# A feed-forward block on one core: x loaded plainly in 32-partition strips and transposed by VectorE in 32x32 blocks

## The chip, the core and the metric

The kernel runs on one NeuronCore of a Trainium2 chip. The metric is the device time of one execution, in microseconds (us). A profiled execution leaves a trace of every instruction; its "span" runs from the first to the last instruction. Engines are TensorE (PE: matmuls, with its weight loads shown apart as PEld), VectorE (DVE), ScalarE (ACT), GpSimd (POOL) and SyncE (SP, which here only issues DMAs and waits). Each engine works through its own instructions in order and waits for others by semaphores.

## The reference

```
x: 1 x 2048 x 512, w_gate and w_up: 512 x 1376, w_down: 1376 x 512, all bf16
g = silu(x @ w_gate)
u = x @ w_up
return (g * u) @ w_down
```

S = 2048 tokens, D = 512, F = 1376. A matmul on TensorE contracts over partitions, so for the first two products x has to stand in SBUF with D on the partitions, that is, transposed; D is cut into four slices of 128, numbered dk.

## The kernel before, in words

**Tiles.** The tokens are worked on in four chunks c of 512 (SC). F is cut into ten full tiles of 128 (ft = 0 to 9) and a rest of 96. For each chunk and each full tile there is a pair of groups: G (gate) and U (up), each of four 128x512 matmuls (dk = 0 to 3) that accumulate in one of eight PSUM banks. ScalarE turns a finished G bank into silu in SBUF; VectorE multiplies that by the finished U bank and writes the product to hT_sb. After the ten pairs of a chunk comes one group X of four matmuls (gate rest and a part of the up rest, L325), with two silus and one product. After all chunks, two groups Y do what is left of the up rest, and then 16 groups O multiply hT_sb by w_down (L353), one per 128 tokens; VectorE copies each O bank out and SyncE stores it.

**Order.** The order is written out by hand. Planning functions (plan_pair, plan_x, plan_y) append groups to one list, which TensorE works through, and append operations to act_ops and dve_ops, which ScalarE and VectorE work through strictly in that order. Every VectorE operation raises the semaphore s_D by one, so a wait for "operation n of VectorE" is a wait for all operations before it too. Before a group may write its bank, the readers of the group eight places earlier must be done (free). A weight slab or a piece of x is waited for by its own DMA semaphore (need).

**Loads.** SyncE issues, in this order: the first 256 tokens of x as two plain loads into xn_sb (tokens on partitions); tokens 256 to 511 ("x0b") as a DMA transpose straight into xT_sb (load_x, L79); the weight slabs from tile 1 on, each as a gate part and an up part (load_w, L84), of 1, 2, 3 and 4 tiles; the rest of w_up; chunks 1 to 3 of x, one DMA transpose each; w_down in two loads. ScalarE issues slab 0 (wg0 and wu0) before its table load. Row d of a weight goes to partition d % 128, slice d // 128 ("(k p) f").

**The head.** TensorE starts with four dummy matmuls of 512 columns on constants (warm, L296). GpSimd builds an identity. As the two plain pieces of x arrive, TensorE transposes them with the identity (L304, two 128x128 blocks to a bank), and VectorE (slices 0 and 1) and ScalarE (slices 2 and 3) copy the banks into xT_sb. Three dummies of 128 columns follow, and then the first pair is worked in pieces of tokens as they are there: 128, 128, then 256.

Of the kernel before, what the change touches and what calls it, by code (L numbers as in the profile page):

```python
# [5 lines left out]
ALU = mybir.AluOpType  # L6
BF16 = mybir.dt.bfloat16
FP32 = mybir.dt.float32

N_WARM = 4  # L10
N_FILL = 3


def bass_standalone__swiglu_ffn__prompt_kernel(nc, x, w_gate, w_up, w_down, out):
    _, S, D = x.shape
    F = w_gate.shape[1]
    P = 128
    KD = D // P
    NFF = F // P
    NFT = NFF + 1  # L20
    F_LAST = F - NFF * P
    SC = 512
    NSC = S // SC
    TPC = SC // P
    NST = S // P
    LASTA = 384
    HT = SC // 2
    NXN = HT // P
    NB = 8
    NSG = 4  # L30
    NOS = 3
# [2 lines left out]
    xf = x[0]  # L34
# [3 lines left out]
    UPH = F + 32  # L38
# [4 lines left out]
    with ExitStack() as es:  # L43
        sb = lambda name, shape, dt: es.enter_context(nc.sbuf_tensor(name, shape, dt))
        ps = lambda name, shape, dt: es.enter_context(nc.psum_tensor(name, shape, dt))
        sem = lambda name: es.enter_context(nc.semaphore(name))
# [9 lines left out]
        o_sb = [sb(f"o_sb{i}", [P, D], BF16) for i in range(NOS)]  # L56
        banks = [ps(f"bank{i}", [P, 512], FP32) for i in range(NB)]

        xn_sb = sb("xn_sb", [P, NXN, D], BF16)
        ident = sb("ident", [P, P], BF16)  # L60

        s_I = sem("s_I")
        s_P = sem("s_P")
        s_A = sem("s_A")
        s_D = sem("s_D")
# [3 lines left out]
        def load_sem(name):  # L69
            loads[name] = sem(f"s_{name}")  # L70
            return loads[name]
# [3 lines left out]
        zero_c = nc.const_aps.tensor(0.0, [P, 4], FP32)  # L75


        def load_x(eng, name, t0, t1):
            eng.dma_start_transpose(  # L79
                xT_sb[:, :, t0:t1], xf[t0:t1, :]  # L80
            ).then_inc(load_sem(name), 16)

        def load_w(eng, name, src, base, f0, f1):
            eng.dma_start(  # L84
                w_sb[:, :, base + f0:base + f1],
                src[:, f0:f1].rearrange("(k p) f -> p k f", p=P),
            ).then_inc(load_sem(name), 16)

        slabs = [(0, 1), (1, 2), (2, 4), (4, 7), (7, NFT)]
# [2 lines left out]
        def load_slab(eng, a, b):  # L92
            load_w(eng, f"wg{a}", w_gate, 0, a * P, min(b * P, F))
            load_w(eng, f"wu{a}", w_up, UPH, a * P, min(b * P, F - 32))

        def loads_on_scalar(act):
            load_slab(act, *slabs[0])

        def loads_on_sync(sp):
            for i in range(NXN):  # L100
                sp.dma_start(xn_sb[:, i, :], xf[i * P:(i + 1) * P, :]).then_inc(load_sem(f"xn{i}"), 16)
            load_x(sp, "x0b", HT, SC)
            for a, b in slabs[1:]:
                load_slab(sp, a, b)
            load_w(sp, "wut", w_up, F - (F - 32), F - 32, F)
            for c in range(1, NSC):
                load_x(sp, f"x{c}", c * SC, (c + 1) * SC)
            sp.dma_start(
                wd_sb[:, 0:NFF, :], w_down[0:NFF * P, :].rearrange("(k p) d -> p k d", p=P)
            ).then_inc(load_sem("wd"), 16)  # L110
            sp.dma_start(wd_sb[0:F_LAST, NFF, :], w_down[NFF * P:F, :]).then_inc(load_sem("wdt"), 16)
# [7 lines left out]
        def add_group(kind, **what):  # L119
            g = dict(kind=kind, at=len(groups), bank=banks[len(groups) % NB], readers=[], **what)  # L120
            groups.append(g)
            return g

        def add_op(eng, g, **what):
            n_read[eng] += 1
            op = dict(g=g, at=n_read[eng], **what)
            (act_ops if eng == "A" else dve_ops).append(op)
            g["readers"].append((eng, op["at"]))
            return op

        def tview(bank):
            return bank[:, 0:P].bitcast(BF16).rearrange("p (k t) -> p k t", k=2)

        sg_reader = []
        n_sg = 0
        h_ready = {}
# [1 line left out]
        def plan_pair(c, ft):  # L138
            nonlocal n_sg
            gg = add_group("G", c=c, ft=ft)  # L140
            gu = add_group("U", c=c, ft=ft)
            b = n_sg % NSG
            free = sg_reader[n_sg - NSG] if n_sg >= NSG else 0
            a = add_op("A", gg, kind="silu", out=sg_sb[b][:, :], src=gg["bank"][:, :], free=free)
            d = add_op(
                "D", gu, kind="mul", out=hT_sb[:, ft, c * SC:(c + 1) * SC], a=sg_sb[b][:, :],
                b=gu["bank"][:, :], after=a["at"],
            )
            sg_reader.append(d["at"])
            h_ready[c] = d["at"]  # L150
            n_sg += 1

        def yblk(c):
            return (0, 64) if c % 2 == 0 else (64, 128)
# [4 lines left out]
        def plan_x(c):  # L159
            g = add_group("X", c=c)  # L160
            y0, y1 = yblk(c)
            add_op("A", g, kind="silu", out=sgx_sb[c][96:128, :], src=g["bank"][64:96, :], free=0)
            a = add_op("A", g, kind="silu", out=sgy_sb[c][y0:y1, :], src=g["bank"][0:64, :], free=0)
            add_op(
                "D", g, kind="mul", out=hT_sb[64:96, NFF, c * SC:(c + 1) * SC],
                a=sgx_sb[c][96:128, :], b=g["bank"][96:128, :], after=a["at"] - 1,
            )
            y_after[c] = a["at"]
# [8 lines left out]
                )  # L177
                t_ready[c] = d["at"]

        xt_ready = {}  # L180
        for i in range(NXN):
            for h, eng in enumerate("DA"):
                g = add_group("T", i=i, h=h)
                op = add_op(
                    eng, g, kind="copy", out=xT_sb[:, 2 * h:2 * h + 2, i * P:(i + 1) * P],
                    src=tview(g["bank"]), stored=(None, 0),
                )
                xt_ready[i, h] = (eng, op["at"])
        NT = len(groups)

        for c in range(NSC):
            for ft in range(NFF):
                plan_pair(c, ft)
            plan_x(c)
        for pi in range(NSC // 2):
            plan_y(pi)
# [22 lines left out]
            for i in range(NOS):  # L219
                sp.wait_ge(s_out[i], 16 * n_store[i])  # L220

        def on_gpsimd(pool):
            pool.affine_select(
                ident[:, :], ones_w, pattern=[[-1, P]], compare_op=ALU.is_equal, fill=0.0,
                base=0, channel_multiplier=1,
            ).then_inc(s_I, 1)

        def on_scalar(act):
            loads_on_scalar(act)
            act.activation(adummy[:, 0:4], zero_c, ACT.Silu)  # L230
# [10 lines left out]
                act.activation(op["out"], op["src"], fn).then_inc(s_A, 1)  # L241

        def on_vector(dve):
            for op in dve_ops:
                dve.wait_ge(s_P, op["g"]["at"] + 1)
                if op["kind"] == "mul":
                    dve.wait_ge(s_A, op["after"])
                    ins = dve.tensor_tensor(op["out"], op["a"], op["b"], ALU.mult)  # L248
                else:
                    if op["stored"][1]:  # L250
                        dve.wait_ge(*op["stored"])
                    ins = dve.tensor_copy(op["out"], op["src"])  # L252
                ins.then_inc(s_D, 1)

        def on_tensor(pe):
            landed = set()

            def need(name):
                if name not in landed:
                    pe.wait_ge(loads[name], 16)  # L260
                    landed.add(name)
# [3 lines left out]
            def after(eng, n):  # L265
                if n > read[eng]:
                    pe.wait_ge(s_A if eng == "A" else s_D, n)
                    read[eng] = n
# [5 lines left out]

            def gu_matmuls(g, n0, n1):
                c, ft = g["c"], g["ft"]
                if c > 0:
                    need(f"x{c}")
                if c == 0 and n1 > HT:
                    need("x0b")  # L280
                need(("wg" if g["kind"] == "G" else "wu") + str(slab_of[ft]))
                col = (0 if g["kind"] == "G" else UPH) + ft * P
                for dk in range(KD):
                    if c == 0 and dk % 2 == 0:
                        for i in range(n0 // P, min(n1 // P, NXN)):
                            after(*xt_ready[i, dk // 2])
                    ins = pe.matmul(  # L287
                        g["bank"][:, n0:n1], lhsT=w_sb[:, dk, col:col + P],
                        rhs=xT_sb[:, dk, c * SC + n0:c * SC + n1], start=(dk == 0), stop=(dk == KD - 1),
                    )  # L290
                if n1 == SC:
                    ins.then_inc(s_P, 1)
# [3 lines left out]
                    pe.matmul(banks[NB - 1][:, 0:width], lhsT=ones_w, rhs=ones_m[:, 0:width], start=True, stop=True)  # L296

            warm(N_WARM, SC)
            pe.wait_ge(s_I, 1)
            for g in groups[:NT]:  # L300
                need(f"xn{g['i']}")
                for j in range(2):
                    dk = 2 * g["h"] + j
                    ins = pe.transpose(tview(g["bank"])[:, j, :], xn_sb[:, g["i"], dk * P:(dk + 1) * P], ident[:, :])  # L304
                ins.then_inc(s_P, 1)
            warm(N_FILL, P)

            first = groups[NT:NT + 2]
            for i in range(NXN):
                for g in first:  # L310
                    gu_matmuls(g, i * P, (i + 1) * P)
            for g in first:
                gu_matmuls(g, HT, SC)

            for g in groups[NT + 2:]:
                free(g)
                kind = g["kind"]
                if kind in "GU":
# [38 lines left out]
                    ins.then_inc(s_P, 1)  # L357

        on_sync(nc.sync)
        on_gpsimd(nc.gpsimd)  # L360
        on_scalar(nc.scalar)
        on_tensor(nc.tensor)
        on_vector(nc.vector)
# [28 lines left out]
```

## Time and profile before

| what | value |
|---|---|
| device time, median of 3 runs | 123.11 us (122.13, 123.11, 123.12) |
| the profiled execution: span | 121.8 us; its time outside the span is not given |
| PE busy | 117.7 us, 97% of the span, 560 matmuls |
| DVE busy | 44.3 us, 36%, 66 instructions |
| ACT busy | 31.1 us, 26% |
| DMA, busy share | about 9 tenths and more from 3 to 24 us, then nearly none until the stores |

How to read it: busy time of an engine counts only if the engine is on the chain of work that ended last. The trace gives this chain, the waits of each engine with what ended them, groups of equal instructions by line and by shape (count, busy time, mean duration), the DMA issues with the time from issue to landing, and a timeline. A matmul's recorded duration runs past the start of the next one, since matmuls are pipelined; the distance between starts is what a matmul costs.

### The profile page before, as it was taken

How to read it: one execution, taken by the hardware profiler on the slowest of the kernel's cores; microseconds unless marked ns; L12 is line 12 of the kernel's file. 1: busy time of each engine (PE TensorE's matmuls, PEld its weight loads, DVE VectorE, ACT ScalarE, POOL GpSimd, SP SyncE). 2: the span in 40 equal slices, each digit the busy share in tenths (PEclk: the TensorE clock that was granted, in tenths of full speed). 3: DMA queues.
4: the chain of work that ended last, by engine and by line, in shares of the span. 5: the costliest groups of instructions: out<-in, count | busy, mean ns of one | idle time of the engine just before them, and what ended most of it. 6: DMA issues, size and time to landing. Idle time of an engine off the chain costs nothing.

```text
span 121.8 us, 1422 instructions
## 1 busy us (share of the span) xinstructions
PE 117.7 (97%) x560; PEld 55.1 (45%) x570; DVE 44.3 (36%) x66; ACT 31.1 (26%) x53; POOL 0.5 (0%) x5
## 2 busy tenths in 40 slices
PE   6899999999999999999999999999999999999993
PEld 1674444444444444444444444444444444444452
DVE  0112443444443344442353444368224223322420
ACT  3313233353233353323353323330000000000001
POOL 1000000000000000000000000000000000000000
PEclk9999999999999999999999999999999999999999
DMA  3999999920000000000000000000121121112112
GB/s 100 219 333 357 268 211 154 348 93 0 0 0 0 0 5 0 0 0 3 3 0 0 0 5 0 0 0 0 54 76 43 48 85 44 43 45 84 43 43 86
DMA packets 17254, 8.51 MB, mean 70 GB/s; under 512 B 10496, under 2 KB 17248, under 8 KB 17248
## 3 DMA queue, kind: packets, MB, share of 16 engines
q1 hardware_dynamic: 16192, 8.16, 25.9%
q10 hardware_dynamic: 1056, 0.26, 1.1%
q8 instruction: 4, 0.07, 0.2%
q14 instruction: 2, 0.02, 0.0%
HBM read 4.49 MB, written 2.10 MB: 54 GB/s over the span
## 4 chain that ended last, share of the span: by engine, by line
PE 94%; DMA 3%; issue 1%; ACTq 0%; DVE 0%
PE bank L287 58%; PE bank L353 31%; DMA w_sb<-in_w_up_dram 3%; PE bank L325 3%; PE bank L336 2%; ACTq L84 0%; DVE o_sb L252 0%
## 5 line engine op out<-in xcount | busy, mean ns | idle before, releaser
L287 PE MATMUL bank<-xT_sb,w_sb 128*128 128x512 bf16 (+2 forms) x329 | 71.5, 378 | 0.7 <-DMA w_sb<-in_w_up_dram 0.3
L287 PEld LDWEIGHTS bank<-xT_sb,w_sb 128*128 128x128 bf16 x336 | 33.5, 102 | 37.9 <-DMA w_sb<-in_w_up_dram 0.6
L248 DVE TENSOR_TENSOR hT_sb<-sg_sb,bank 128x512 bf16<-128x512 f32 x40 | 27.5, 687 | 43.0 <-PE bank L287 42.5
L353 PE MATMUL bank<-wd_sb,hT_sb 128*128 128x512 bf16 (+4 forms) x184 | 38.1, 366 | 0.2
L241 ACT ACTIVATE sg_sb<-bank 128x512 f32<-128x512 f32 x40 | 23.8, 596 | 43.3 <-PE bank L287 43.2
L353 PEld LDWEIGHTS bank<-wd_sb,hT_sb 128*128 128x128 bf16 (+1 forms) x187 | 17.8, 98 | 20.7 <-DVE hT_sb L248 0.4
L252 DVE CAST o_sb<-bank 128x512 bf16<-128x512 f32 (+1 forms) x16 | 10.7, 667 | 25.4 <-PE bank L353 25.3
L241 ACT ACTIVATE o_sb<-bank 128x384 bf16<-128x384 f32 x1 | 0.5, 490 | 38.2 <-PE bank L353 38.2
L325 PE MATMUL bank<-xT_sb,w_sb 128*128 128x512 bf16 x16 | 4.1, 379 | 0.0
L248 DVE TENSOR_TENSOR hT_sb<-sgx_sb,bank 32x512 bf16<-32x512 f32 x4 | 2.8, 693 | 3.5 <-ACT sgx_sb L241 3.5
L241 ACT ACTIVATE sgx_sb<-bank 32x512 f32<-32x512 f32 x4 | 2.3, 587 | 4.5 <-PE bank L325 4.5
L296 PE MATMUL bank<-const-bfloat16-1.0 128*128 128x512 bf16 (+1 forms) x7 | 2.4, 489 | 0.8 <-PEq L377 0.8
L248 DVE TENSOR_TENSOR hT_sb<-sgy_sb,bank 64x512 bf16<-64x512 f32 x4 | 2.7, 685 | 0.1
L325 PEld LDWEIGHTS bank<-xT_sb,w_sb 128*128 128x128 bf16 x16 | 1.6, 98 | 1.9
L241 ACT ACTIVATE sgy_sb<-bank 64x512 f32<-64x512 f32 x4 | 2.4, 589 | 0.1
L252 DVE COPY xT_sb<-bank 128x256 bf16<-128x256 bf16 x2 | 0.6, 292 | 3.9 <-PE bank L304 3.9
L336 PE MATMUL bank<-xT_sb,w_sb 128*64 128x512 bf16 x16 | 1.9, 382 | 0.0
L230 ACT ACT_TABLE_LOAD x1 | 1.3, 1283 | 1.9 <-issue 1.9
L304 PE MATMUL bank<-ident,xn_sb 128*128 128x128 bf16 x8 | 1.2, 302 | 0.5 <-DMA xn_sb<-in_x_dram 0.4
L304 PEld LDWEIGHTS bank<-ident,xn_sb 128*128 128x128 bf16 x8 | 0.7, 127 | 1.7 <-issue 1.3
L296 PEld LDWEIGHTS bank<-const-bfloat16-1.0 128*128 128x128 bf16 x7 | 0.8, 136 | 1.4 <-issue 1.4
L336 PEld LDWEIGHTS bank<-xT_sb,w_sb 128*64 128x64 bf16 x16 | 0.8, 109 | 1.0 <-DVE hT_sb L248 0.4
(7 smaller groups left out, 1.7 us busy)
## 6 DMA issues: line engine op xcount, KB each, us to landing
out_dram<-o_sb SPq DMA_DIRECT2D x15, 128.0 KB, 1.7
wd_sb<-in_w_down_dram SPq DMA_DIRECT2D x1, 1280.0 KB, 7.3
w_sb<-in_w_gate_dram SPq DMA_DIRECT2D x1, 480.0 KB, 5.7
w_sb<-in_w_up_dram SPq DMA_DIRECT2D x1, 448.0 KB, 6.2
w_sb<-in_w_gate_dram SPq DMA_DIRECT2D x1, 384.0 KB, 4.3
w_sb<-in_w_up_dram SPq DMA_DIRECT2D x1, 384.0 KB, 4.8
xn_sb<-in_x_dram SPq DMA_DIRECT2D x2, 128.0 KB, 2.3
w_sb<-in_w_gate_dram SPq DMA_DIRECT2D x1, 256.0 KB, 3.7
```

What stands on the lines that cost most here:

```text
L230: act.activation(adummy[:, 0:4], zero_c, ACT.Silu)
L241: act.activation(op["out"], op["src"], fn).then_inc(s_A, 1)
L248: ins = dve.tensor_tensor(op["out"], op["a"], op["b"], ALU.mult)
L252: ins = dve.tensor_copy(op["out"], op["src"])
L287: ins = pe.matmul(g["bank"][:, n0:n1], lhsT=w_sb[:, dk, col:col + P], rhs=xT_sb[:, dk, c * SC + n0:c * SC + n1], start=(dk == 0), stop=(dk ...
L296: pe.matmul(banks[NB - 1][:, 0:width], lhsT=ones_w, rhs=ones_m[:, 0:width], start=True, stop=True)
L304: ins = pe.transpose(tview(g["bank"])[:, j, :], xn_sb[:, g["i"], dk * P:(dk + 1) * P], ident[:, :])
L325: ins = pe.matmul(g["bank"][:, :], lhsT=w_sb[:, dk, XC0:XC0 + P], rhs=xT_sb[:, dk, c * SC:(c + 1) * SC], start=(dk == 0), stop=(dk == KD - 1),
L336: ins = pe.matmul(g["bank"][y0:y1, :], lhsT=w_sb[:, dk, YC0:YC0 + 64], rhs=xT_sb[:, dk, c * SC:(c + 1) * SC], start=(dk == 0), stop=(dk == ...
L353: ins = pe.matmul(g["bank"][:, 0:c1 - c0], lhsT=hT_sb[0:K, fk, t * P:(t + 1) * P], rhs=wd_sb[0:K, fk, c0:c1], start=(fk == 0), stop=(fk == ...
```

## The change

The DMA transposes, TensorE's transposes with their copies, the identity and its semaphore are gone. In their place:

- **Load.** Each piece of x is loaded plainly as four strips q, one per 32 partitions. Strip q holds the columns 128q to 128q+127 of x; partition 32q + t, group g of xl_sb holds token 32g + t. Tokens 0 to 255 (x0a) and 256 to 511 (x0b) come as two strips from SyncE and two from ScalarE each; chunks 1 to 3 as four strips each from SyncE. The four strips of a piece count on one semaphore.
- **Turn.** One VectorE transpose per piece of 64 or 128 tokens moves 32x32 blocks: output partition 32q + r, slice k, token t is column 128q + 4r + k of the input. So partition p, slice k holds D-index 4p + k, and the gate and up weights are loaded to match ("(p k) f"). VectorE waits for all four strips of a piece ahead of its first turn.
- **Place of the turns.** Chunk 0 is turned at the start, in pieces of 64, 64, 128, 128, 128 tokens. The four turns of chunk c+1 stand in VectorE's order behind the products of pairs 6, 7, 8 and 9 of chunk c, and ahead of the product of X.
- **Waits.** Each G or U group waits for the turns of all its tokens (x_ready) before its first matmul.
- **Head.** Six dummies of 512 columns instead of four, then the three of 128. wg0 is now issued by SyncE and wu0 by ScalarE, each between the strips of x0a and x0b. The first pair runs as G on 64, 64, 128 tokens, U on 256, then G and U on 128 and again on 128.

```diff
-N_WARM = 4
+N_WARM = 6
...
-        def load_x(eng, name, t0, t1):
-            eng.dma_start_transpose(
-                xT_sb[:, :, t0:t1], xf[t0:t1, :]
-            ).then_inc(load_sem(name), 16)
+        def load_x(eng, name, t0, t1, strips):
+            if name not in loads:
+                load_sem(name)
+            for q in strips:
+                eng.dma_start(
+                    xl_sb[TB * q:TB * (q + 1), t0 // TB:t1 // TB, :],
+                    xf[t0:t1, q * P:(q + 1) * P].rearrange("(g t) m -> t g m", t=TB),
+                ).then_inc(loads[name], 16)
...
-                src[:, f0:f1].rearrange("(k p) f -> p k f", p=P),
+                src[:, f0:f1].rearrange("(p k) f -> p k f", k=KD),
...
         def loads_on_scalar(act):
-            load_slab(act, *slabs[0])
+            load_x(act, "x0a", 0, HT, (2, 3))
+            load_w(act, "wu0", w_up, UPH, 0, P)
+            load_x(act, "x0b", HT, SC, (2, 3))
 
         def loads_on_sync(sp):
-            for i in range(NXN):
-                sp.dma_start(xn_sb[:, i, :], xf[i * P:(i + 1) * P, :]).then_inc(load_sem(f"xn{i}"), 16)
-            load_x(sp, "x0b", HT, SC)
+            load_x(sp, "x0a", 0, HT, (0, 1))
+            load_w(sp, "wg0", w_gate, 0, 0, P)
+            load_x(sp, "x0b", HT, SC, (0, 1))
...
-                load_x(sp, f"x{c}", c * SC, (c + 1) * SC)
+                load_x(sp, f"x{c}", c * SC, (c + 1) * SC, range(KD))
...
+        def plan_turn(name, t0, t1):
+            n_read["D"] += 1
+            dve_ops.append(dict(kind="turn", name=name, t0=t0, t1=t1, at=n_read["D"]))
+            for t in range(t0, t1, TB):
+                x_ready[t] = n_read["D"]
...
+        for t0, t1 in ((0, 64), (64, P), (P, HT)):
+            plan_turn("x0a", t0, t1)
+        for t0, t1 in ((HT, HT + P), (HT + P, SC)):
+            plan_turn("x0b", t0, t1)
         for c in range(NSC):
             for ft in range(NFF):
                 plan_pair(c, ft)
+                if c + 1 < NSC and ft >= NFF - TPC:
+                    t0 = (c + 1) * SC + (ft - NFF + TPC) * P
+                    plan_turn(f"x{c + 1}", t0, t0 + P)
             plan_x(c)
...
         def on_vector(dve):
+            turned = set()
             for op in dve_ops:
+                if op["kind"] == "turn":
+                    if op["name"] not in turned:
+                        dve.wait_ge(loads[op["name"]], 16 * KD)
+                        turned.add(op["name"])
+                    g0, g1 = op["t0"] // TB, op["t1"] // TB
+                    dve.transpose(
+                        xT_sb[:, :, op["t0"]:op["t1"]].rearrange("p k (g t) -> p g k t", t=TB),
+                        xl_sb[:, g0:g1, :].rearrange("p g (r k) -> p g k r", k=KD),
+                    ).then_inc(s_D, 1)
+                    continue
...
                 need(("wg" if g["kind"] == "G" else "wu") + str(slab_of[ft]))
+                for t in range(c * SC + n0, c * SC + n1, TB):
+                    after("D", x_ready[t])
...
-            first = groups[NT:NT + 2]
-            for i in range(NXN):
-                for g in first:
-                    gu_matmuls(g, i * P, (i + 1) * P)
-            for g in first:
-                gu_matmuls(g, HT, SC)
+            g, u = groups[0:2]
+            for n0, n1 in ((0, 64), (64, P), (P, HT)):
+                gu_matmuls(g, n0, n1)
+            gu_matmuls(u, 0, HT)
+            for n0, n1 in ((HT, HT + P), (HT + P, SC)):
+                for gr in (g, u):
+                    gu_matmuls(gr, n0, n1)
```

More of the change, by code (lines that the diff above doesn't have):

```diff
@@ L8 @@
 FP32 = mybir.dt.float32
-N_WARM = 4
+N_WARM = 6
 N_FILL = 3
+TB = 32
 def bass_standalone__swiglu_ffn__prompt_kernel(nc, x, w_gate, w_up, w_down, out):
@@ L27, in bass_standalone__swiglu_ffn__prompt_kernel @@
     HT = SC // 2
-    NXN = HT // P
+    NG = S // TB
     NB = 8
@@ L57, in bass_standalone__swiglu_ffn__prompt_kernel @@
         banks = [ps(f"bank{i}", [P, 512], FP32) for i in range(NB)]
-        xn_sb = sb("xn_sb", [P, NXN, D], BF16)
-        ident = sb("ident", [P, P], BF16)
-        s_I = sem("s_I")
+        xl_sb = sb("xl_sb", [P, NG, P], BF16)
         s_P = sem("s_P")
@@ L129, in add_op @@
             return op
-        def tview(bank):
-            return bank[:, 0:P].bitcast(BF16).rearrange("p (k t) -> p k t", k=2)
         sg_reader = []
@@ L151, in plan_pair @@
             n_sg += 1
+        x_ready = {}
+        def plan_turn(name, t0, t1):
[3 more added lines that the diff above has]
+                x_ready[t] = n_read["D"]
         def yblk(c):
@@ L178, in plan_y @@
                 t_ready[c] = d["at"]
-        xt_ready = {}
-        for i in range(NXN):
[L182 to L189, printed above, removed]
+        for t0, t1 in ((0, 64), (64, P), (P, HT)):
+            plan_turn("x0a", t0, t1)
+        for t0, t1 in ((HT, HT + P), (HT + P, SC)):
+            plan_turn("x0b", t0, t1)
         for c in range(NSC):
@@ L220, in on_sync @@
                 sp.wait_ge(s_out[i], 16 * n_store[i])
[L222 to L226, printed above, removed]
         def on_scalar(act):
@@ L276, in gu_matmuls @@
                 c, ft = g["c"], g["ft"]
[L277 to L280, printed above, removed]
                 need(("wg" if g["kind"] == "G" else "wu") + str(slab_of[ft]))
+                for t in range(c * SC + n0, c * SC + n1, TB):
+                    after("D", x_ready[t])
                 col = (0 if g["kind"] == "G" else UPH) + ft * P
                 for dk in range(KD):
-                    if c == 0 and dk % 2 == 0:
-                        for i in range(n0 // P, min(n1 // P, NXN)):
-                            after(*xt_ready[i, dk // 2])
                     ins = pe.matmul(
@@ L298, in on_tensor @@
             warm(N_WARM, SC)
[L299 to L305, printed above, removed]
-            warm(N_FILL, P)
-            first = groups[NT:NT + 2]
-            for i in range(NXN):
-                for g in first:
-                    gu_matmuls(g, i * P, (i + 1) * P)
-            for g in first:
-                gu_matmuls(g, HT, SC)
-            for g in groups[NT + 2:]:
+            warm(N_FILL, P)
+            g, u = groups[0:2]
[5 more added lines that the diff above has]
+                    gu_matmuls(gr, n0, n1)
+            for g in groups[2:]:
                 free(g)
@@ L359, in bass_standalone__swiglu_ffn__prompt_kernel @@
         on_sync(nc.sync)
-        on_gpsimd(nc.gpsimd)
         on_scalar(nc.scalar)
```

## The prediction

> **What bounds the kernel now.** I read the page first: the span, then the shares of the chain that ended last.
>
> ```profile
> span 121.8 us, 1422 instructions
> ...
> PE 94%; DMA 3%; issue 1%; ACTq 0%; DVE 0%
> PE bank L287 58%; PE bank L353 31%; DMA w_sb<-in_w_up_dram 3%; PE bank L325 3%; PE bank L336 2%; ACTq L84 0%; DVE o_sb L252 0%
> ```
>
> TensorE sets the end: its matmul lines are 94% of the chain, and the only other entry of size is one weight load. So a step counts only if TensorE starts later, runs slower or is held. The chain in order of time tells where that load stands.
>
> ```profile
> 1.30 4.11 DMA w_sb<-in_w_up_dram
> 5.41 0.05 issue
> 5.45 5.75 PE bank L287 x30
> ```
>
> The first up slab lands at 5.41; 0.04 us later TensorE goes on, and from there the chain shows no wait of more than 0.05. All that the change can win lies before about 9 us; afterwards it can only lose.
>
> Two places decide. The first is the change of chunk, here from chunk 0 to 1 in the timeline (start, length, engine, line):
>
> ```profile
> 24.62 0.69 DVE L248 TENSOR_TENSOR hT_sb<-sg_sb,bank 128x512 bf16<-128x512 f32 x1 [1.04 <-PE bank L287]
> 24.64 0.81 PE L325 MATMUL bank<-xT_sb,w_sb 128*128 128x512 bf16 x3
> ...
> 25.29 1.89 PE L287 MATMUL bank<-xT_sb,w_sb 128*128 128x512 bf16 x8
> ```
>
> The first line is VectorE's product for the last full pair of chunk 0. TensorE meanwhile runs the four X matmuls (the first began just before this window) and begins chunk 1 at 25.29. The product ends at 25.31: nothing of chunk 1 hangs on it today. The second place is the head. These groups by shape (count, busy, mean ns) serve both:
>
> ```profile
> L287 PE MATMUL bank<-xT_sb,w_sb 128*128 128x512 bf16 x305 | 67.9, 381 | 0.4
> ...
> L252 DVE CAST o_sb<-bank 128x512 bf16<-128x512 f32 x15 | 10.4, 692 | 23.7 <-PE bank L353 23.6
> ...
> L287 PE MATMUL bank<-xT_sb,w_sb 128*128 128x256 bf16 x8 | 1.9, 421 | 0.0
> ...
> L252 DVE COPY xT_sb<-bank 128x256 bf16<-128x256 bf16 x2 | 0.6, 292 | 3.9 <-PE bank L304 3.9
> ...
> L252 DVE CAST o_sb<-bank 128x128 bf16<-128x128 f32 x1 | 0.3, 293 | 1.7 <-PE bank L353 1.7
> ```
>
> The 256-wide matmuls, all in the head, last longer than the 512-wide ones. The timeline has the same in spacing: between the first silu (7.80) and the first product (8.66) lie four 256-wide matmuls, 0.215 each; between later silus (11.68, 13.40) lie eight 512-wide, also 0.215 each. So TensorE ran at half speed in the head, up to the matmul that starts at 9.27, though the page's clock row shows 9 throughout.
>
> **The change of chunk.** A turn of 128 tokens is one VectorE transpose of 512 elements per partition. No row of before is a transpose. The two CASTs give VectorE's price: (692 - 293)/384 = 1.04 ns per element, 0.16 us fixed. By these a turn is 0.16 + 512 x 1.04 = 0.69 us. The COPY, bf16 to bf16, ran at half that per element (292 - 160 over 256): 0.43 us, my low end. The input is read in steps of four elements, which no row shows; twice the rate per element is my high end, 1.23 us. I take 0.69: the COPY reads densely and the turn does not. The Trainium skill, in VectorE: DVE Perf Modes, section The three transpose paths, gives VectorE 311 ns for a 128x128 bf16 transpose in 32x32 blocks; no run here shows one, and with 384 more elements at 1.04 that is an estimate of 0.71 us, which would make the sum below 0.06 us larger.
>
> The turns for chunk c+1 stand in VectorE's queue behind the products of pairs 6 to 9 of chunk c. Behind the first three there is room: products come every 1.73 us, product plus turn take 1.38. The fourth stands behind the product of pair 9, and chunk c+1's first gate group waits for all four turns. At the change shown: product ends 25.31, turn 0.02 later until 26.02, TensorE released after the 0.04 seen above, at 26.06 instead of 25.29. The cover is the X group alone, and the product uses it up. Stall: turn + 0.09 = 0.78 us. The product starts 0.20 us after the first X matmul at all three changes (24.63, 42.76, 60.88), so 3 x 0.78 = **+2.35 us** (low 3 x 0.52 = 1.55). At the high end product plus turn are 1.92 against the 1.73 period: VectorE falls 0.19 behind at each of the three pairs, and a stall is 1.23 + 0.09 + 0.57 = 1.9, 5.7 in all. Behind the late turn on VectorE waits the X product, which started at 26.18 for ScalarE's sake: hidden at 0.69.
>
> **The head.** Gone are TensorE's eight transposes (3.12 to about 4.2), two copies each on VectorE and ScalarE, the mask on GpSimd (0.29) and the 0.5 us wait for the up slab. Two dummies of 0.43 each come in; all nine now end near 3.7 with nothing to wait for, so they cost nothing if the data is later than that. The DMA issues of before (size, us to landing):
>
> ```profile
> xn_sb<-in_x_dram SPq DMA_DIRECT2D x2, 128.0 KB, 2.3
> ...
> w_sb<-in_w_gate_dram ACTq DMA_DIRECT2D x1, 128.0 KB, 2.6
> w_sb<-in_w_up_dram ACTq DMA_DIRECT2D x1, 128.0 KB, 4.1
> ```
>
> An issue holds its queue for 0.4 to 0.5 us. So the two x0a strips on each queue are issued by 1.75, each queue's first weight slab by 2.3, the x0b strips by 3.2. With 2.3 to 2.6 from issue, x0a is complete at 3.6 to 3.9; the first turn (64 tokens, 0.43) ends at 4.3. The slabs, issued at about 1.75, land at 4.35 by 2.6 and 5.85 by 4.1; before, the first 512 KB were in at 5.41, with part of x0b moving beside them, so I take 4.7. At half speed the gate group's 256 tokens then take three pieces of 4 x 0.107 (the weight loads there take 0.10 to 0.15 each, so a narrower matmul is no quicker), until 6.0, the up group's 256 tokens 0.86, until 6.85. x0b (256 KB more) landed at 6.1 before, as a transpose; I take 5.9, 0.5 either way; its first turn ends at 6.6, the second at 7.3, and 16 matmuls of 0.107 end at 8.55. Before, pair 0 was through its last matmul 0.25 before its product, near 8.4. **Head: about +0.1** at unchanged speed, between -0.4 and +0.5; I write 0 and keep both ends.
>
> **Work beside.** ScalarE issues five DMAs instead of two, to 3.3; its table load (1.28) and dummy (0.21) end near 4.8, and its first silu was at 7.80. SyncE's slabs keep their places (first at 3.07 before, about 3.15 after). It issues x1 to x3 as twelve strips, each near 0.5 instead of three transposes in 9.5. w_down, last in the queue, landed at 27.2 and is used at 81.6: no cost. x in 256-byte pieces: the ACT queue moved 1056 packets in 1.1% of 16 engines' 121.8 us, 20 ns each, so x1's 2048 packets take 2.6 us. The last slab landed near 13.5; with up to 1 us of delay x1 is in by 17.1; the first of its turns stands behind the product that ends at 20.14. It hides; the cover is 3 us. Chunks 1 to 3 lose the transposes' waits, which were nil.
>
> **Sum.** +2.35 on the span: 121.8 becomes 124.15. The page prints no time of the profiled execution outside its span; the lowest run (122.13) lies 0.3 above the span, the median (123.11) 1.3. On the median: **125.45**.
>
> **Rivals.** *One: full speed comes earlier.* Between 5.45 and 9.27 TensorE worked 3.8 us at half speed, so at most 1.9 us can be won, and somewhat less because x0b's turns end at 7.3. With 1.7 won the time is 123.75, not slower by the bound below. For it: 2.9 us of unbroken dummies from 0.84. Against: before also ran from 3.12 to 5.0 with few gaps and was not yet fast at 5.45; after stands idle from 3.7 to 4.7. It decides from 1.2 us won (2.35 - 1.2 is 1% of the median). The Trainium skill, TensorE: Matmul & The Clock Gate, Part 1, says that the array runs at half rate until it was busy through a window of about 3.4 us, whose phase is free of the kernel's start. By that rule, the switch at 9.27, 3.8 us after 5.45, agrees; the phase would move between runs, and more dummies help only when no gap falls into the window. I give this 0.22.
>
> *Two: the turn is cheap.* At the COPY's rate the stalls are 1.55: 124.7; only a turn under 0.31 us would leave 1.2 in all. 0.12, a quarter of it under that bound.
>
> *Three: turns too long, or x1 late.* A turn over 1.04 us (1.73 - 0.69) puts VectorE behind: up to 128.8. x1 landing after 21.2 (26.06 less four turns and three products) shifts the first change one for one. 0.08 together.
>
> *Four: the head wins more than the stalls cost.* That needs one's full 1.9 and an x0b a microsecond early as well, some 2.9 in all. Over 1% faster: 0.06.
>
> **Numbers.** The forecast as worked out, stalls of about 0.8 and a head within half a microsecond, has 0.52: 124.9 to 126.2. A measurement of this kernel can tell about 1% (1.2 us) from no change. Faster: 0.06. Same: rival one mostly, 0.19, a quarter of two, 0.03, and 0.02 of the forecast's edge: 0.24. Slower: 0.70. The range from 123.4 (rival one with a head 0.35 early) to 126.9 (head +0.5 and turns of near 1 us: 3 x 0.3 more) leaves out three's long end and four.
>
> **What would show it.** After the change VectorE should have 17 turns: 15 of some 0.69 us and two of some 0.43. TensorE should show a wait on VectorE of about 0.8 us three times, behind the X groups. The first gate matmul should stand near 4.7, pair 0 end near 8.5, and the 256-wide matmuls still be spaced 0.215. x1 should land before 20. I am wrong if the stalls are absent, because the last turn ends before the X group does, or if the matmuls from 5 us on come at full speed.

## The result, and the profile after

The changed kernel takes 126.46 us (median of four runs, 126.20 to 127.06) where the kernel before took 122.83 beside it: a ratio of 1.035 (95% interval 1.030 to 1.041). A second measurement gave 125.89 against 122.42, ratio 1.030 (1.026 to 1.035). Slower was forecast, by 2.35 us; by the medians it is 3.5 to 3.6. (The ratios in this document stand with their intervals as recorded; the quotients of the medians differ from them by up to 0.7%.)

| | before | after |
|---|---|---|
| span of the profiled execution | 121.8 | 124.9 |
| its time | not given | 126.23 |
| PE busy | 117.7 | 117.6 |
| DVE busy | 44.3 | 53.8 |

The time lies 1.3 above the span in each of the four runs after (126.23 over 124.9, 127.06 over 125.8). All later executions of before lie 1.2 to 1.3 above their spans too, so the profiled execution of before took about 123.1. That is the median that the prediction was set on, but it is one of the longer executions of its kernel, whose medians beside the later runs were 122.2 to 122.8.

The profile page of the changed kernel: span, chain by engine, chain by line.

```profile
span 124.9 us, 1451 instructions
...
PE 89%; DVE 4%; DMA 3%; ACTq 2%; issue 1%
PE bank L293 56%; PE bank L353 30%; DMA xl_sb<-in_x_dram 3%; DVE xT_sb L251 2%; DVE hT_sb L259 2%; PE bank L336 1%; ACTq L81 1%; PE bank L325 1%; ACTq L87 0%; DVE o_sb L263 0%
```

TensorE has as much work as before, but VectorE is now on the chain with 4%, by two lines: the turn (L251) and the product (L259). In order of time (start, length, what) the chain shows where:

```profile
3.23 3.22 DMA xl_sb<-in_x_dram
6.44 0.02 issue
6.47 0.72 DVE xT_sb L251
7.19 0.05 issue
7.24 4.33 PE bank L293 x24
...
25.41 0.69 DVE hT_sb L259
26.10 0.64 DVE xT_sb L251
26.73 0.14 issue
26.87 7.07 PE bank L293 x32
```

The first lines are the head: TensorE now waits for x0b (landed 6.44) and its first turn, where before it waited for the up slab. The last four are the first change of chunk: product, then turn, then TensorE. The other two are alike, with TensorE going on at 45.79 and 64.71. The timeline of TensorE alone, from the same stretch of the changed kernel, has the gap behind the X group:

```profile
24.78 0.59 PE L293 MATMUL bank<-xT_sb,w_sb 128*128 128x512 bf16 x2
25.21 1.03 PE L325 MATMUL bank<-xT_sb,w_sb 128*128 128x512 bf16 x4
26.87 1.45 PE L293 MATMUL bank<-xT_sb,w_sb 128*128 128x512 bf16 x6 [0.63 <-DVE xT_sb L251]
```

The last X matmul starts at 25.86 and the next matmul at 26.87: 1.01 us instead of the usual 0.216, so 0.79 lost, at each of the three changes. That is 2.38 us. The rest of the span's 3.1 is the head: the first matmul of pair 1's up group starts at 10.53 instead of 9.75, 0.78 later.

VectorE's turns by shape (count, busy, mean ns) in the changed kernel:

```profile
L251 DVE STREAM_TRANSPOSE xT_sb<-xl_sb 128x512 bf16<-128x512 bf16 x15 | 10.4, 700 | 1.3 <-DMA xl_sb<-in_x_dram 1.3
...
L251 DVE STREAM_TRANSPOSE xT_sb<-xl_sb 128x256 bf16<-128x256 bf16 x2 | 0.8, 424 | 3.8 <-DMA xl_sb<-in_x_dram 3.8
```

Now the head. These are stretches of the changed kernel: stretch, its length, busy us (and count) of PE, PEld, DVE, ACT, POOL, then the granted clock, DMA share and GB/s.

```profile
3.61:7.02 3.41, 1.40 (x18) 0.82 (x16) 1.92 (x4) 1.49 (x2) 0.00 (x0) 1.00 1.10 238
7.02:10.43 3.41, 3.19 (x20) 2.29 (x21) 1.44 (x3) 0.60 (x1) 0.00 (x0) 0.50 1.03 297
10.43:13.00 2.57, 2.52 (x12) 1.17 (x12) 0.69 (x1) 1.14 (x2) 0.00 (x0) 1.00 1.06 339
```

From 3.61 to 7.02 the array ran at full speed, from 7.02 to 10.43 at half (0.50), and then at full. The spacing of the matmuls says the same: 256-wide ones 0.11 apart near 5.6 us, 128-wide ones 0.107 apart from 7.4 on, 512-wide ones 0.427 apart up to 10.2. So full speed had come early and was lost again at 7.02, between the landing of x0b (6.44) and the first matmul on its tokens (7.24). In the stretch ahead of the loss (3.61 to 7.02) TensorE had little to do: its 16 matmuls hold it for 0.9 of the 3.41 us, by the spacing of their starts; the rest is the wait for the gate slab (to 4.66), a short one for the third turn, and the wait for x0b from 5.85 on, which ends at 7.24.

### The profile page after: what moved, and what is told of

It reads as the page before. It is cut to its first block, busy times and chain, and to the rows that moved or that the text cites. A ratio compares the mean times of both kernels' runs of the same rounds, so it can differ in the third digit from the quotient of the medians.

```text
span 124.9 us, 1451 instructions
## 1 busy us (share of the span) xinstructions
PE 117.6 (94%) x562; PEld 54.3 (43%) x572; DVE 53.8 (43%) x81; ACT 30.6 (25%) x51; POOL 0.2 (0%) x4
## 4 chain that ended last, share of the span: by engine, by line
PE 89%; DVE 4%; DMA 3%; ACTq 2%; issue 1%
PE bank L293 56%; PE bank L353 30%; DMA xl_sb<-in_x_dram 3%; DVE xT_sb L251 2%; DVE hT_sb L259 2%; PE bank L336 1%; ACTq L81 1%; PE bank L325 1%; ACTq L87 0%; DVE o_sb L263 0%
## 5 line engine op out<-in xcount | busy, mean ns | idle before, releaser
L293 PE MATMUL bank<-xT_sb,w_sb 128*128 128x512 bf16 (+3 forms) x338 | 71.3, 371 | 4.4 <-DVE xT_sb L251 3.1
L293 PEld LDWEIGHTS bank<-xT_sb,w_sb 128*128 128x128 bf16 x344 | 33.0, 101 | 42.5 <-DVE xT_sb L251 5.0
L259 DVE TENSOR_TENSOR hT_sb<-sg_sb,bank 128x512 bf16<-128x512 f32 x40 | 27.5, 688 | 37.3 <-PE bank L293 35.6
L251 DVE STREAM_TRANSPOSE xT_sb<-xl_sb 128x512 bf16<-128x512 bf16 (+1 forms) x17 | 11.1, 668 | 5.1 <-DMA xl_sb<-in_x_dram 5.1
L302 PE MATMUL bank<-const-bfloat16-1.0 128*128 128x512 bf16 (+1 forms) x9 | 3.0, 515 | 0.8 <-PEq L376 0.8
L259 DVE TENSOR_TENSOR hT_sb<-sgx_sb,bank 32x512 bf16<-32x512 f32 x4 | 2.8, 692 | 1.6 <-ACT sgx_sb L241 1.6
L259 DVE TENSOR_TENSOR hT_sb<-sgy_sb,bank 64x512 bf16<-64x512 f32 x4 | 2.7, 685 | 0.1
L325 PEld LDWEIGHTS bank<-xT_sb,w_sb 128*128 128x128 bf16 x16 | 1.6, 98 | 1.9
```

Source lines behind the costliest of these rows:

```text
L251: dve.transpose(xT_sb[:, :, op["t0"]:op["t1"]].rearrange("p k (g t) -> p g k t", t=TB), xl_sb[:, g0:g1, :].rearrange("p g (r k) -> p g k r ...
L293: ins = pe.matmul(g["bank"][:, n0:n1], lhsT=w_sb[:, dk, col:col + P], rhs=xT_sb[:, dk, c * SC + n0:c * SC + n1], start=(dk == 0), stop=(dk ...
L325: ins = pe.matmul(g["bank"][:, :], lhsT=w_sb[:, dk, XC0:XC0 + P], rhs=xT_sb[:, dk, c * SC:(c + 1) * SC], start=(dk == 0), stop=(dk == KD - 1),
```

## The experiments

Two questions: are the gaps at the changes of chunk due to the place of the last turn, and what makes the head late? The medians below are us; the kernel before, run beside them, had medians between 122.2 and 122.4 (single runs 121.4 to 123.5). The head's speed differs between executions of one kernel, and the spans with it, so places are judged by gaps, heads by medians.

### a_early: no turn behind the last product

```diff
-                if c + 1 < NSC and ft >= NFF - TPC:
-                    t0 = (c + 1) * SC + (ft - NFF + TPC) * P
-                    plan_turn(f"x{c + 1}", t0, t0 + P)
+                for j in {NFF - 4: (0,), NFF - 3: (1,), NFF - 2: (2, 3)}.get(ft, ()):
+                    if c + 1 < NSC:
+                        t0 = (c + 1) * SC + j * P
+                        plan_turn(f"x{c + 1}", t0, t0 + P)
```

> The changed kernel with one thing moved: the four turns of a chunk stand behind the products of pairs 6, 7, 8 and 8 instead of 6, 7, 8 and 9, so nothing of the next chunk stands behind the product of pair 9. Place theory (each change of chunk costs turn + 0.09 us because the last turn follows the last product): the three gaps of 1.01 us between matmul starts go back to 0.22, and the span falls by 3 x 0.79 = 2.4 us, to about 122.5. Rival, VectorE has too much to do in the last four pairs (product plus turn against a period of 1.73 us): the two turns now behind pair 8 push the product of pair 9 back and the gaps stay at 0.5 us or more, a gain of at most 1.5. Rival, the strips of x for the next chunk arrive late: the gap at the first change stays and the other two go.

Measured: 124.46 (123.05 to 125.87, the other four up to 124.89), ratio 1.023 (1.017 to 1.030). The profiled execution's span is 121.7, below the expected 122.5, for in it full speed came at 8.6 rather than 10.4. The timeline of TensorE at the first change, and then the lines of the waits (total us, times, longest) for turns by TensorE and its weight loads:

```profile
24.41 1.03 PE L326 MATMUL bank<-xT_sb,w_sb 128*128 128x512 bf16 x4
25.27 2.10 PE L294 MATMUL bank<-xT_sb,w_sb 128*128 128x512 bf16 x9
```

```profile
PE bank L294 <- DVE xT_sb L252: 1.7, 2, 1.2
...
PEld bank L294 <- DVE xT_sb L252: 1.0, 1, 1.0
```

The group of chunk 1 follows the X group without a gap (25.27 is 0.86, four matmuls, after 24.41), and what is left of waits for turns lies in the head. All three gaps are gone: the place theory holds and neither rival does. The medians fall by 1.4 to 2.0, less than the 2.4 us of the gaps, with heads that differ from execution to execution; against the profile of after_again below, whose head is alike (first matmul of pair 1's up group at 9.98, here 9.73), the span is 2.6 us shorter, of which 0.25 is that head. With two turns behind pair 8, the product of pair 9 began at 24.71, a tenth later than without them, and no group of chunk 1 waited for it.

### a_late2: two turns behind the last product

```diff
+                for j in {NFF - 4: (0,), NFF - 3: (1,), NFF - 1: (2, 3)}.get(ft, ()):
```

> The changed kernel with the third turn moved the other way, so that two turns of 128 tokens stand behind the product of pair 9. Place theory: each gap at a change of chunk grows by one turn, from 1.01 to about 1.66 us (0.65 from one turn's start to the next); the span by 3 x 0.65 = 2 us against the same head. If something else held TensorE there (the arrival of x, the banks), the gaps stay at 1.01.

One execution: 128.03, span 126.7. VectorE and TensorE at the first change (the second line is two turns):

```profile
25.43 0.69 DVE L260 TENSOR_TENSOR hT_sb<-sg_sb,bank 128x512 bf16<-128x512 f32 x1 [1.04 <-PE bank L294]
26.03 1.30 DVE L252 STREAM_TRANSPOSE xT_sb<-xl_sb 128x512 bf16<-128x512 bf16 x2
...
27.48 1.24 PE L294 MATMUL bank<-xT_sb,w_sb 128*128 128x512 bf16 x5 [1.22 <-DVE xT_sb L252]
```

The gaps between matmul starts are 1.60 us at all three changes, 0.59 more than with one turn (0.65 expected). So the stall grows with the number of turns behind the last product: none, 0; one, 0.79; two, 1.39.

### b_warm6: the dummies alone

```diff
-N_WARM = 4
+N_WARM = 6
```

on the kernel before.

> The kernel before with six dummies at the start instead of four, nothing else. If unbroken work from 0.8 to 3.4 us is enough to bring full speed early, and the short waits behind it do not lose it, the span falls by 1 us or more, since the kernel before worked at half speed up to 9.3 us. If the wait for the up slab near 5 us loses it again, the same or up to 0.4 us slower, for the transposes start 0.4 us later.

Measured: 121.02 (120.80 to 121.40), ratio 0.992 (0.989 to 0.995). Two dummies make the kernel before 1.1 us faster, and narrow its spread from 1.5 us (the twelve runs beside it) to 0.6 (eight runs). From its profile, the span, TensorE's timeline and the 256-wide matmuls by shape:

```profile
span 119.8 us, 1426 instructions
```

```profile
0.84 2.72 PE L296 MATMUL bank<-const-bfloat16-1.0 128*128 128x512 bf16 x6 [0.84 <-PEq L377]
3.35 1.00 PE L304 MATMUL bank<-ident,xn_sb 128*128 128x128 bf16 x8
4.19 0.34 PE L296 MATMUL bank<-const-bfloat16-1.0 128*128 128x128 bf16 x3
4.37 0.38 PE L287 MATMUL bank<-xT_sb,w_sb 128*128 128x128 bf16 x4
5.01 4.24 PE L287 MATMUL bank<-xT_sb,w_sb 128*128 128x128 bf16 x29 [0.26 <-DMA w_sb<-in_w_up_dram]
```

```profile
L287 PE MATMUL bank<-xT_sb,w_sb 128*128 128x256 bf16 x8 | 1.0, 274 | 0.0
```

In this head one thing follows another: dummies, TensorE's transposes, dummies, first matmuls, and the wait for the up slab is the only long gap. The 256-wide matmuls last 274 ns where they lasted 421: full speed came at 4.03 and stayed, and pair 1 begins at 6.91 instead of 8.41. So one edit of the change is a gain on the kernel before, and against a kernel before that has the six dummies too the rest of the change costs some 5 us, not 3.6 (1.030 to 1.035 against 0.992).

### a_warm4: the change without the two dummies

```diff
-N_WARM = 6
+N_WARM = 4
```

> The changed kernel with four 512-wide dummies at the start instead of six. If the dummies are what brings full speed at 3.6 us, then without two of them the first groups run at half speed (64- and 128-wide matmuls 0.107 apart), which is hidden, since x0b sets the pace from 7.2 us on; full speed then comes at a similar time as before, 9 to 11 us, and the span changes by less than 0.5 us either way: the additional dummies gained nothing. Rival, the dummies carry the head: 1 us or more slower.

Measured: 126.52 (125.83 to 126.58), ratio 1.036 (1.032 to 1.040). That is within the range of the changed kernel in its two measurements (125.5 to 127.1): in the changed head the two dummies bring nothing that can be measured. In this profile the 128-wide matmuls are 0.107 apart and full speed comes at about 10.9.

### a_fill and a_early_fill: dummies in the wait for x0b

```diff
             gu_matmuls(u, 0, HT)
+            warm(6, SC)
```

> The changed kernel with six 512-wide dummy matmuls put between the up group's first 256 tokens and the wait for x0b, where TensorE stood idle for 1.4 us. Gap theory (the idle time makes the array fall back to half speed for the stretch of 3.41 us that follows): with the gap filled the array stays at full speed, the 16 matmuls on x0b's tokens take 0.06 us instead of 0.107 each and the next four 0.22 instead of 0.43, together 1.5 us less, a span near 123.4. Phase theory (the slow stretch comes where it comes, whatever stands before it): the dummies run partly at half speed, the slow stretch stays, and the span is the same or up to 1 us longer.

> The kernel with the turns moved off the last pair, and the six dummies put into the wait for x0b. If the two repairs add, the median is that of the moved turns (124.5) less what the filling is worth where it keeps or brings full speed, up to 1.5 us: 123 to 124.5. Where the wait for the first gate slab is long (the first gate matmul came between 4.7 and 5.6 us so far) the array is at half speed anyway and the dummies themselves run slowly: no gain there.

Measured: a_fill 125.18 (125.09 to 126.90, three runs near 125.1 and two near 126.8); a_early_fill 124.07 (123.94 to 124.40), ratio 1.0145 (1.010 to 1.019), 0.4 below a_early by the medians. The gain is less than the gap theory had at its best, and the profile of a_fill, from one of its longer executions (126.68), shows why. The gate slab landed at 5.60 there, so TensorE stood idle for over 2 us first; the array was at half speed when the filling began, and six dummies held TensorE from 7.33 to 9.24, while the first turn of x0b was done at 7.99. Full speed came during the dummies, at 8.6. What the later matmuls won, the dummies had taken. In a_early_fill's profile it went the same way, with full speed from about 9.1. That fits the gap theory, and the phase theory as well; these two runs don't decide.

### a_early_w9 and a_early_keep: no long gap at the start

```diff
-N_WARM = 6
+N_WARM = 9
```

on a_early, and on a_early_fill.

> The kernel with the turns moved off the last pair, and nine 512-wide dummies at the start instead of six, so that TensorE works without a gap until about 4.7 to 5 us. Gap theory: full speed comes at 4.2 to 7 us in every run; it may be lost again through the wait for x0b (about 1 to 1.4 us), as in the changed kernel's profile. Median between 123 and 124.5, less spread than the 2.8 us of the moved turns alone.

> Both: nine dummies at the start and six in the wait for x0b, turns off the last pair. Gap theory: TensorE has no long gap any more, full speed comes by 4.2 to 7 us and stays; what is left of the head is the arrival of x0b and its two turns, pair 0 ends near 8.3 us at full speed, where the kernel before with six dummies ended it at 6.9. So 1.2 to 1.5 us above that kernel's 121.0: a median of 122.2 to 122.6. Phase theory (gaps do not matter): as the moved turns alone, near 124.5, with the same spread.

Measured: 122.78 (122.56 to 123.27) and 122.81 (122.58 to 123.16), ratios 1.0044 (1.0019 to 1.0069) and 1.0040 (1.0015 to 1.0066). Three more dummies, bridging the wait for the gate slab, are worth 1.7 us by the medians on the moved turns, and the spread falls from 1.8 us (2.8 with the one execution at 125.87) to 0.7. The first is 0.2 below what was expected, the second 0.2 above. The phase theory, in which gaps do not matter, forecast 124.5 with the spread of the moved turns, and does not hold. TensorE in the head of a_early_keep:

```profile
0.77 4.04 PE L303 MATMUL bank<-const-bfloat16-1.0 128*128 128x512 bf16 x12 [0.77 <-PEq L378]
4.78 1.12 PE L294 MATMUL bank<-xT_sb,w_sb 128*128 128x64 bf16 x16
5.74 1.47 PE L303 MATMUL bank<-const-bfloat16-1.0 128*128 128x512 bf16 x6
7.35 1.86 PE L294 MATMUL bank<-xT_sb,w_sb 128*128 128x128 bf16 x18
```

The groups on x0b's tokens run 0.056 apart, at full speed. The filling adds nothing here: in the profile of a_early_w9 TensorE waits 1.0 us for x0b (6.25 to 7.30) and is still at full speed after it. So the gap that mattered is the one before the first gate matmul, and not every gap of 1 us loses the speed. What remains against b_warm6 is 1.8 us by the medians and 1.5 by the two profiles' spans. The profiles account for it by the arrival of x0b: 6.56 instead of 5.77, then two turns of 0.64 to 0.71, so that pair 0's last matmul starts at 8.35 instead of 6.60; b_warm6 then waits some 0.2 us for a weight slab before pair 1.

### h_pe: the head alone undone

```diff
         def loads_on_scalar(act):
-            load_x(act, "x0a", 0, HT, (2, 3))
-            load_w(act, "wu0", w_up, UPH, 0, P)
-            load_x(act, "x0b", HT, SC, (2, 3))
+            load_slab(act, *slabs[0])
...
-            load_x(sp, "x0a", 0, HT, (0, 1))
-            load_w(sp, "wg0", w_gate, 0, 0, P)
-            load_x(sp, "x0b", HT, SC, (0, 1))
+            for i in range(NXN):
+                sp.dma_start(xn_sb[:, i, :], xf[i * P:(i + 1) * P, :]).then_inc(load_sem(f"xn{i}"), 16)
...
+                        ins = pe.transpose(
+                            tview(g["bank"])[:, j, :],
+                            xn_sb[:, g["i"], :].rearrange("t (p k) -> t k p", k=KD)[:, dk, :], ident[:, :],
+                        )
```

> The head alone undone: chunk 0 comes as four plain loads of 128 tokens with whole rows and is transposed by TensorE (copies by VectorE and ScalarE), wg0 and wu0 are issued first by ScalarE, six dummies as in the change but not the three narrow ones; chunks 1 to 3 come as strips and are turned by VectorE behind pairs 6, 7, 8 and 8. If the head's strips and their order in the queues are what the change still loses, this comes to the kernel before with six dummies: 121.0, within 0.7. If the turns and strips of the later chunks cost something too (VectorE, the DMA queue), it stays near the moved turns alone, 123 to 124.5.

Measured: 121.83 (121.61 to 123.76; eight of eleven runs at most 121.92, three above 123.4), ratio 0.997 (0.994 to 1.001); span 120.5. It is 0.8 above b_warm6, and pair 1 begins at 7.62 in its profile instead of 6.91: 0.7 of that is its own head. So strips and turns of chunks 1 to 3, once off the last product, cost nothing that shows. (The expectation had 121.0 within 0.7 for this case; 121.83 lies just outside, and well below the other case's 123 to 124.5.) What the change still lost lies in the head, in the loads and turns of chunk 0 and TensorE's waits for them. Here x's first 512 tokens came in rows of 1024 bytes, with slab 0 ahead in the other queue, and all that the head loads had landed by 5.74; in the changed kernel the same bytes took until 6.44.

### after_again

> The changed kernel unchanged, beside the same runs of the kernel before as the next one: a second measurement of the change, 126 to 127, and a second look at where full speed sets in.

Measured: 125.89 (125.51 to 126.52), just below the 126 to 127 expected; the profiled execution took 125.67. TensorE in its head:

```profile
0.77 3.04 PE L302 MATMUL bank<-const-bfloat16-1.0 128*128 128x512 bf16 x9 [0.77 <-PEq L376]
4.64 1.90 PE L293 MATMUL bank<-xT_sb,w_sb 128*128 128x64 bf16 x16 [0.83 <-DMA w_sb<-in_w_gate_dram]
7.14 5.16 PE L293 MATMUL bank<-xT_sb,w_sb 128*128 128x128 bf16 x29 [0.61 <-DVE xT_sb L251]
```

In this profile full speed comes once, at 9.41, and no early stretch exists, though the gap ahead of the first gate matmul was 1.15 between starts, as in the other profile (1.16). With that gap, early full speed comes in one execution and not in another. The gaps at the changes of chunk are 1.01 again. The span is 124.3. Before, full speed came at 9.36, so here the speed really is unchanged, and the head costs little: pair 1 begins 0.40 later than before (8.82 for 8.41), and its up group 0.23 later (9.98 for 9.75).

## Why the prediction was right and wrong

**The change of chunk: right.** The price of a turn, read off the two CASTs as 0.69 and 0.43 us, measured 0.700 and 0.424; the end taken from the COPY's faster rate and the doubled one did not come about. The stall was forecast as 0.78 and measured as 0.79, the sum as 2.35 and measured as 2.38; removing and doubling the turns behind the last product moved it as forecast. That it fits to the hundredth is luck: the turn starts 0.08 before the product's end (26.02 against 26.10), not 0.02 after it, and TensorE goes on 0.15 after the turn's end (26.72 to 26.87), not 0.04. The 0.71 that the prediction estimated from the Trainium skill, VectorE: DVE Perf Modes, section The three transpose paths, is near the 0.700 as well.

**The head: wrong.** This is the term that was mis-sized: "about +0.1 at unchanged speed, between -0.4 and +0.5; I write 0". It measured +0.78 between the first two profiles, and 1.1 to 1.25 as the rest of the two measured increases (3.47 and 3.63) after the 2.38. Two steps of it failed, and what the term was measured against adds the rest. The range's upper end, too, was made of other things, a head of +0.5 and turns near 1 us.

First, x0b. It was taken to land at 5.9, 0.5 either way; of the nine profiles in which it is loaded as strips it landed between 6.35 and 6.6 in seven, and near 7.2 in two. The prediction set out from the moment at which the DMA transpose of before had landed; but ahead of it now lay 256-byte pieces throughout. The first gate matmul, forecast near 4.7, came at 4.64 to 5.65. In the forecast's path the first turn of x0b, done at 6.6, was hidden behind TensorE's work on the first 256 tokens, which was to last until 6.85. That work was done earlier, at 5.85 in the first profile and at 6.33 in after_again's, where the 64-wide matmuls were 0.053 apart at half speed and not 0.107; and the turn ended later, at 7.18 and 7.08. So TensorE waited for x0b, which the forecast did not have. With this, pair 1 begins 0.50 later than before (8.92 for 8.41) in the changed kernel's first profile, where the forecast had some 0.1.

Second, "unchanged speed". The array's speed differed in most of the head. In the profile it had full speed from 3.6 to 7.0, through matmuls that were waiting for data anyway, and half speed from 7.0 to 10.4, through the 16 matmuls on x0b and most of pair 1's gate group; before, half speed ended at 9.36. That is the other 0.28 of the 0.78.

The moment of full speed is not the same in every execution (3.6 and then 10.4 in one profile of the changed kernel, 9.4 in the other), and the forecast took that of before's one profile as the kernel's own. Where it was nearly the same (9.41 against 9.36), the head cost 0.23, not far from the forecast's +0.1. Where full speed is there on both sides (a_early_keep against b_warm6), late data isn't hidden by slow matmuls any more, and the head costs 1.5 to 1.8. And the one profile of before was of a long execution, about 123.1 where its medians are 122.2 to 122.8, so the measured increases are larger than the difference of the profiles.

**Rival one** (full speed comes earlier) named the right mechanism, and its point against ("after stands idle from 3.7 to 4.7") was what decided. It left out that the kernel before with six dummies, whose TensorE has transposes to do in that time, would keep the speed. The dummies' gain is real, 1.1 us, on the kernel before; in the changed kernel it is lost in the waits. The Trainium skill, TensorE: Matmul & The Clock Gate, Part 1, gives windows of about 3.4 us with a phase of their own; the stretches of 3.41 us in the trace, and the onset at 3.6, 4.0, 5.9, 9.4 or 10.4 us in different profiles, agree.

**The x1 cover** was forecast as 3 us and was 1.7: x1 landed at 19.13, not by 17.1, and the first of its turns began at 20.84. The price of 20 ns per 256-byte piece was too low. In stretches of the changed kernel in which mostly weights of 768 bytes a piece (first), and then mostly pieces of x (second and third) were moved, the last two columns are DMA share and GB/s:

```profile
9.07:11.79 2.72, 2.67 (x10) 1.04 (x9) 0.88 (x2) 0.86 (x2) 0.00 (x0) 0.75 1.03 321
...
16.60:19.13 2.53, 2.53 (x13) 1.16 (x12) 1.31 (x2) 0.60 (x1) 0.00 (x0) 1.00 1.31 179
19.13:22.51 3.38, 3.33 (x16) 1.57 (x16) 1.93 (x4) 1.20 (x2) 0.00 (x0) 1.00 1.08 164
```

At 164 to 179 GB/s a chunk of x takes 2.9 to 3.2 us instead of the 2.6 that the sum had, and the slabs ahead of it were in at 16.0 rather than 14.5. It stayed hidden, so rival three's price did not come due. The DMA transposes of before moved no faster (160 GB/s from 16 to 20 us), so this is not what the change costs in the later chunks.

**What stays open.** Why x0b is late isn't settled: larger pieces and another order of the queues were tried only together, in h_pe, where the same bytes were in 0.7 us sooner. Its lateness with strips is read from landings. Which share of busy time keeps the array at full speed isn't settled either: TensorE worked 0.9 us of the 3.41 from 3.61 on in the changed kernel and lost it; it worked 2.2 us of the 3.41 that follow the onset at 5.89 in a_early_w9 and kept it. Why three of h_pe's eleven executions are 1.6 to 2 us longer than the rest isn't known.

## What to carry to other kernels

An operation that feeds the next stage should not stand, in an in-order queue, behind the last operation of this stage: here moving one turn by one place took away three gaps of 0.79 us, with no other work changed. In these runs the gain of warming the array up was kept only where real work or more dummies followed without a long wait, so judge dummies together with the arrival of the first data. And where a change bundles several edits, measure each alone: the dummies alone give 121.0, faster than both kernels, while all the rest of the change costs some 5: 2.4 in stalls, the rest in the head.

## What the runs showed that was not expected

- The kernel before spreads over 121.4 to 123.5 us; with two more dummies, which bring full speed at 4.0 us in the profile, 0.6 us of spread are left. Most of the spread would then be the moment at which full speed sets in; no profile of its other executions shows that.
- Seven of the twelve profile pages have no clock row, though the spacing shows a change of speed in each of them; in the other five it reads 9 in the first stretch although 512-wide matmuls are 0.427 us apart there. Only from the first recorded change on does it tell the speed (0.50 from 7.02 to 10.43). Spacing of starts is the safer reading.
- TensorE's transposes ran 0.056 us apart in b_warm6 once full speed had come, and in h_pe likewise, like matmuls of the same width.
- Issues of x strips held SyncE for 0.95 to 1.5 us each for x1, against 0.4 to 0.5 for the first strips of the kernel. Several loads were outstanding by then; SyncE had nothing else to do.
